# Weight blocks issued at other places of the SyncE queue, and other widths of the column chunks

## The chip, the cores and the metric

The kernel runs on one NeuronCore of one Trainium2 chip. The metric is the device time of one execution in microseconds (us), the median of three runs. A core has TensorE (matrix products), VectorE, ScalarE and GpSimd (elementwise work), and SyncE, which in this kernel only issues transfers. The page of the profile calls them PE (PEld: its weight loads), DVE, ACT, POOL and SP.

## The reference

Chunk-wise attention over 64-token blocks, then an MLP with the SoLU activation and layer norm, then an MLP with PReLU. The change lies in the last part. Cut to it:

```python
# attention and the first MLP give x: 4608 tokens x 512
def _moe2_ref(x, w_in, w_out, alpha):          # d_model 512, d_ff 2048
    h = x @ w_in
    g = np.maximum(h, 0.0) + alpha * np.minimum(h, 0.0)
    return (g @ w_out).astype(np.float32)
```

Everything is float32, and the result has shape 4608 x 512.

## The kernel before, in words

**Phase 1** (`phase1`) computes attention and the first MLP, leaves its result `y` transposed in DRAM (tiles `yd`), and writes the two weights of the second MLP to DRAM in a prepared form (`wid` for `w_in`, `wod` for `w_out`). **Phase 2** (`phase2`) is the second MLP and what the change touches.

Phase 2 forms each matrix product by Strassen's scheme in Winograd's form: both matrices are cut into 2 x 2 quadrants, and seven products of sums of quadrants (`p1` to `p7`) take the place of eight. Each operand is split in a high and a low part, and a product is high*high + high*low + low*high. So each block of a weight holds high and low parts of seven operands: 14336 bytes a partition, 1792 KB a block. Each weight has eight such blocks (`NB2`), tiles `w20` to `w27`. Blocks 0 and 1 lie at the left of the on-chip memory, where room is free early (`NL = 2`), blocks 2 to 7 at the right, in memory that phase 1 holds to its end.

**First product, x @ w_in, with PReLU.** The tokens come as pairs (`PAIRS` = 2304 columns, half of the tokens each side), in six stripes of 384 columns (`SG`, loop `s`). For each stripe the four quadrants of `y` are loaded (`load_y`, four transfers of 384 KB, SyncE queue), and for each of the eight blocks of the weight there is one *unit* (`unit`, loop `b`), 48 in all. A unit runs 7 products of 6 matmuls of 384 columns, in the order p1, p6, p5, p7, p2, p3, p4, in four PSUM banks hx, hy, hz, hv, which alternate between two sets from unit to unit; p2, p3 and p4 accumulate onto hx, hz and hv of the same unit after these have been read. Four results come out, called 22, 11, 12 and 21 in the order in which they are made. Each gets a tile `g` out of a pool of seven (line 787), is passed through PReLU (ScalarE's `ng` and `g`, VectorE's L802) and is stored to DRAM tiles `gd` by SyncE (192 KB each, `store`, L807). The stores of 22 and 11 stand at the end of a unit, those of 12 and 21 in the next unit, behind its second product (`late`). A tile `g` can be written again when its store has landed.

**Second product, g @ w_out.** The 2304 columns are cut in chunks (`CHUNKS`, line 38). A chunk has two groups of products (p1, p5, p6, p7 and then p2, p3, p4), and each group four *pieces* j, two blocks of the weight each. `load_g` loads the quadrants a, b, c, d of a piece (only c and d in the second group); `prepare` forms the sums and splits on ScalarE and VectorE; `multiply` runs one *step*: 12 matmuls of the chunk's width, for one product of one piece. 5 chunks x 28 steps are 140 steps. The first piece (0, 0, 0) is loaded and prepared during the last stripe (tiles `fa` to `fd`, `fhi`, `flo`); the others use pools that reuse the memory of the first product (tiles `ra` to `rd`, `rhi`, `rlo`, `rt`; two buffers each of a to d).

**What sets the order.** All transfers of phase 2 are issued by SyncE, in program order, and go through one hardware queue; ScalarE has another queue for phase 1's stores of `y`. SyncE is in order: a transfer that waits (for its data, for its buffer, or for the transfer eight places back on SyncE's and ScalarE's queues, which shares its semaphore) holds all behind it. In the kernel before, blocks 2 to 7 of the first weight are issued together at the end of phase 1 (line 877), ahead of the y loads of the second stripe and of all stores. In the last stripe, the block of the second weight that takes the place of block b is issued at the end of unit b (line 1027).

Of the kernel before, what the change touches and what calls it, by code (L numbers as in the profile page):

```python
# [34 lines left out]
NS = NT // (2 * SG)  # L35
PAIRS = NT // 2
NB2 = KF2 // 2
CHUNKS = [(0, 256)] + [(p, 512) for p in range(256, PAIRS, 512)]

# [48 lines left out]
def tile_chunk_attention_solu_prelu(  # L90
# [29 lines left out]
    wi_dram = dram.tile([128, NB2, 2, 7, 2, 128], F32, name="wid")  # L120
    wo_dram = dram.tile([128, NB2, 2, 7, 256], F32, name="wod")
# [551 lines left out]
    def add(out, a, b):  # L673
        nc.vector.tensor_tensor(out=out, in0=a, in1=b, op=ALU.add)  # L674
# [7 lines left out]
    def phase2():  # L682
        with ExitStack() as c2:
            def P(name, bufs, side="left", stack=c2, **k):
                return stack.enter_context(tc.tile_pool(name=name, bufs=bufs, side=side, reuse_waits="tile", **k))

            NL = 2
# [9 lines left out]
            def load_w(b, src):  # L697
                W[b] = (wl if b < NL else wr).tile([128, 2, 7, 256], F32R, name=f"w2{b}", tag=f"w{b}")
                if src is wi_dram:
                    nc.sync.dma_start(  # L700
                        out=W[b].bitcast(F32).rearrange("p t i c -> p (t i c)"),
                        in_=src[:, b].rearrange("p t i k c -> p (t i k c)"),
                    )
                else:
                    nc.sync.dma_start(out=W[b].bitcast(F32), in_=src[:, b])
# [15 lines left out]
            def load_y(s):  # L721
                for t in ("11", "12", "22", "21"):
                    r, c = int(t[0]) - 1, int(t[1]) - 1
                    raw[t] = slot(F32 if t == "12" else F32R, f"y{t}")
                    nc.sync.dma_start(
                        out=raw[t].bitcast(F32), in_=y_dram[s][:, 2 * r:2 * r + 2, SG * c:SG * c + SG]
                    )
# [21 lines left out]
            class Unit:  # L749
# [34 lines left out]
                    add(self.v, self.ps["z"], self.u)  # L784

                def f(self, t):
                    self.g[t] = self.tile("g", gp, 7)
                    if t != "11":
                        x, o = {"22": ("v", self.v), "12": ("z", self.u), "21": ("v", self.u)}[t]
                        add(self.g[t], self.ps[x], o)  # L790
# [83 lines left out]
            wr = P("w2r", 1, side="right")  # L874
            ps2.append(P("ps_2r", 1, side="right", space=PSUM))
            gp = P("g2", 1, side="right", stack=ca)
            for b in range(NL, NB2):
                load_w(b, wi_dram)


# [1 line left out]
            GROUPS = (("p1", "p5", "p6", "p7"), ("p2", "p3", "p4"))  # L882
            steps = [(c, g, j, p) for c in range(len(CHUNKS)) for g in range(2) for j in range(4) for p in GROUPS[g]]
            pieces = [(c, g, j) for c in range(len(CHUNKS)) for g in range(2) for j in range(4)]
            start = {x: next(t for t, y in enumerate(steps) if y[:3] == x) for x in pieces}
            src, t4s, ops = {}, {}, {}

            def new(x, tag, dtype=F32R):
                n = CHUNKS[x[0]][1]
                if x == (0, 0, 0):  # L890
                    if tag == "t4":
                        return kp.tile([128, 2, n], dtype, name="t4", tag="t4")
                    return slot(dtype, f"f{tag}")[:, :, :n]
                bufs = dict(t3=1, t2=1, t4=4, hi=4, lo=3).get(tag, 2)
                return rp.tile([128, 2, 512], dtype, name=f"r{tag}", tag=tag, bufs=bufs)[:, :, :n]

            def load_g(x):
                c, g, j = x
                p0, n = CHUNKS[c]
                for tag, t in (("a", "11"), ("b", "12"), ("c", "22"), ("d", "21"))[2 * g:]:  # L900
                    src[x, tag] = new(x, tag, F32 if tag == "b" else F32R)
                    nc.sync.dma_start(
                        out=src[x, tag].bitcast(F32), in_=GD[t][:, 2 * j:2 * j + 2, p0:p0 + n]
                    )
# [13 lines left out]
            def prepare(x, p):  # L918
                a, b, c, d = (src.get((x, t)) for t in "abcd")
                k = x[0], x[2]  # L920
                if p == "p1":
                    low_ = split(x, p, a, a)
                    t3 = src[x, "t3"] = new(x, "t3", F32)
                    dsub(t3, c, b)
                    dsub(b, b, a)
                    low_()
                elif p == "p5":
                    low_ = split(x, p, b, None)
                    t2 = src[x, "t2"] = new(x, "t2", F32)
                    dsub(t2, c, b)  # L930
                    t4 = t4s[k] = new(x, "t4", F32)
                    dsub(t4, d, t2)
                    low_()
                else:
                    f = dict(p6=src.get((x, "t2")), p7=src.get((x, "t3")), p2=d, p3=c, p4=t4s.get(k))[p]
                    split(x, p, f, f if p in ("p2", "p3") else None)()
# [3 lines left out]
            def multiply(t):  # L940
                c, g, j, p = steps[t]
                n = CHUNKS[c][1]
                i, _, key = PRODUCTS[p]
# [12 lines left out]
            def evacuate(t):  # L956
                c, g, j, p = steps[t]
                p0, n = CHUNKS[c]
                while out_:
# [41 lines left out]
            for s in range(NS):  # L1001
                for b in range(NB2):
                    def extra(k):
                        if s + 1 == NS:
                            x = (0, 0, 0)
                            if (b, k) == (0, 3):
                                load_g(x)
                            if k == 2 and 4 <= b:
                                prepare(x, GROUPS[0][b - 4])
                        else:  # L1010
                            if (b, k) == (0, 3):
                                load_y(s + 1)
                            if (b, k) in sums:
                                sum_y(sums[b, k])
                            if (b, k) in early:
                                high_y(s + 1, early[b, k])
                            if (b, k - 1) in early:
                                low_y(s + 1, early[b, k - 1])
                        if s and b == 0:
                            if (8, k) in early:  # L1020
                                high_y(s, early[8, k])
                            if (8, k - 1) in early:
                                low_y(s, early[8, k - 1])

                    prev = unit(s * NB2 + b, s, b, prev, extra)
                    if s + 1 == NS:
                        load_w(b, wo_dram)
            for k in range(3):
                prev.late(k)
# [5 lines left out]
            op = P("o3", 1)  # L1035
            LEAD = 3
            load_g(pieces[1])
            load_g(pieces[2])
            for t in range(4, 4 + LEAD):
                prepare(steps[t][:3], steps[t][3])  # L1040
            for t in range(4, len(steps)):
# [43 lines left out]
```

## Time and profile before

| | |
|---|---|
| median of three runs | 1351.19 us (1347.74 to 1352.4) |
| profiled execution, its own time | 1350.37 us |
| its span, first to last instruction | 1348.6 us |
| TensorE busy | 1271.1 us (94%), mean granted clock 0.976 |
| VectorE, ScalarE, GpSimd busy | 947.5, 689.6, 328.3 us |
| first product's units | 602.3 to 979.6 us of the span |
| second product's steps | 979.5 to 1344.8 us |

The profiled execution lies 0.8 us below the median. Its own time is 1.8 us more than its span. A busy TensorE is not TensorE at its best: matmuls overlap in the records, so lengths are better read from one start to the next. Idle time counts only where the last chain of work runs through it; in phase 2 that is TensorE nearly everywhere. The granted clock is given as a share of 2.4 GHz: 1.0 is full, 0.5 is 1.2 GHz.

### The profile page before, as it was taken

What the parts mean: (1) busy time and instruction counts of PE and PEld (TensorE: products, weight loads), DVE (VectorE), ACT (ScalarE), POOL (GpSimd) and SP (SyncE); (2) the same over time, 40 slices, a digit from 0 to 9 for tenths busy, and PEclk for the clock granted to TensorE, in tenths of its full rate; (3) what the DMA queues carried; (4) which work ended last, traced back from release to release, by engine and by line L of the source; (5) the groups of instructions that cost most, each with busy time, mean ns of one, the idle gap of its engine ahead of it and who ended that gap; (6) DMA issues with size and microseconds to landing.
All of it is one profiled execution on the core that took longest, in us unless ns stands there. A gap on an engine that the chain in (4) does not pass through costs nothing. (4 is left out here: it accounts for less than half of the span.)

```text
span 1348.6 us, 21430 instructions
## 1 busy us (share of the span) xinstructions
PE 1271.1 (94%) x7968; PEld 1157.4 (86%) x7968; DVE 947.5 (70%) x1425; ACT 689.6 (51%) x1140; POOL 328.3 (24%) x309
## 2 busy tenths in 40 slices
PE   4999989999999999994999999999968999999998
PEld 3778779999898889994999999999968888888887
DVE  6986576677777676422777777777756859596783
ACT  5675345555555554332666666666534443444442
POOL 4664254354555643401120202100000000000000
PEclk9799999999999999997999999999978999999999
DMA  9864267576756652539242433436975547483743
GB/s 237 174 158 116 73 165 172 149 172 179 212 165 202 193 170 94 198 113 380 106 159 106 158 124 135 147 112 244 328 247 195 188 151 255 134 274 108 265 134 116
DMA packets 214792, 236.30 MB, mean 175 GB/s; under 512 B 89248, under 2 KB 167072, under 8 KB 212640
## 3 DMA queue, kind: packets, MB, share of 16 engines
q1 hardware_dynamic: 204896, 225.49, 53.5%
q10 hardware_dynamic: 9792, 9.44, 2.1%
q8 instruction: 63, 1.03, 0.3%
q14 instruction: 41, 0.34, 0.1%
HBM read 148.90 MB, written 85.98 MB: 174 GB/s over the span
## 5 line engine op out<-in xcount | busy, mean ns | idle before, releaser
L802 DVE SCALAR_TENSOR_TENSOR g<-ng,nal,g 128x384 f32<-128x384 f32 x192 | 123.6, 644 | 62.2 <-ACT g L680 62.2
L160 PE MATMUL yps<-zh,wo_h 128*128 128x256 f32 x576 | 167.3, 290 | 0.0
L162 PE MATMUL yps<-zh,wo_l 128*128 128x256 f32 x576 | 163.0, 283 | 0.0
L161 PE MATMUL yps<-zl,wo_h 128*128 128x256 f32 x576 | 162.9, 283 | 0.0
L680 ACT ACTIVATE ng<-g 128x384 f32<-128x384 f32 x144 | 75.8, 526 | 150.3 <-DVE g L674 150.3
L763 PE MATMUL hx<-th,w 128*128 128x384 f32 x384 | 113.8, 337 | 16.8 <-ACT s L680 16.8
L763 PE MATMUL hz<-th,w 128*128 128x384 f32 x384 | 114.1, 337 | 2.9 <-DVE wv L674 2.9
L763 PE MATMUL hv<-th,w 128*128 128x384 f32 x384 | 113.7, 336 | 2.6 <-DVE g L674 2.3
L161 PEld LDWEIGHTS yps<-zl,wo_h 128*128 128x128 f32 x576 | 110.5, 192 | 0.1
L160 PEld LDWEIGHTS yps<-zh,wo_h 128*128 128x128 f32 x576 | 110.4, 192 | 0.1
L162 PEld LDWEIGHTS yps<-zh,wo_l 128*128 128x128 f32 x576 | 110.3, 191 | 0.0
L950 PE MATMUL ox<-rhi,w 128*128 128x512 f32 (+1 forms) x312 | 98.1, 379 | 8.3 <-ACT rhi L680 8.3
L950 PE MATMUL oz<-rhi,w 128*128 128x512 f32 (+1 forms) x312 | 96.5, 374 | 0.0
L950 PE MATMUL ov<-rhi,w 128*128 128x512 f32 (+1 forms) x312 | 95.2, 370 | 0.0
L677 POOL TENSOR_TENSOR yt<-y,y 128x384 f32<-128x384 f32 x24 | 28.5, 1208 | 257.7 <-DMA y<-yd 257.7
L680 ACT ACTIVATE rhi<-rt 128x1024 fp32r<-128x1024 f32 (+1 forms) x57 | 56.2, 993 | 65.1 <-DVE rt L677 18.4
L763 PEld LDWEIGHTS hx<-th,w 128*128 128x128 f32 x384 | 71.3, 189 | 17.2 <-ACT s L680 17.2
L481 PE MATMUL h<-wi_h,xh 128*128 128x512 f32 x256 | 72.0, 404 | 8.0 <-ACT xh L467 5.2
L677 DVE TENSOR_TENSOR rlo<-rt,rhi 128x1024 fp32r<-128x1024 f32 (+1 forms) x57 | 64.2, 1137 | 18.1 <-ACT rhi L680 17.9
L680 ACT ACTIVATE g<-g 128x384 f32<-128x384 f32 x144 | 75.2, 522 | 3.1
L950 PEld LDWEIGHTS ox<-rhi,w 128*128 128x128 f32 x312 | 59.3, 195 | 18.7 <-ACT rhi L680 8.5
L763 PEld LDWEIGHTS hz<-th,w 128*128 128x128 f32 x384 | 71.3, 189 | 4.6 <-ACT th L680 4.3
(188 smaller groups left out, 3334.7 us busy)
## 6 DMA issues: line engine op xcount, KB each, us to landing
gd<-g SPq DMA_DIRECT2D x192, 192.0 KB, 1.9
rc<-gd SPq DMA_DIRECT2D x32, 512.0 KB, 4.0
rd<-gd SPq DMA_DIRECT2D x32, 512.0 KB, 5.0
w<-wid SPq DMA_DIRECT2D x8, 1792.0 KB, 14.7
w<-wod SPq DMA_DIRECT2D x8, 1792.0 KB, 9.5
raw<-in_moe_w_out SPq DMA_DIRECT2D x24, 511.8 KB, 3.9
qt<-in_q SPq DMA_DIRECT2D x36, 256.0 KB, 5.2
kbd<-in_k SPq DMA_DIRECT2D x72, 128.0 KB, 5.0
```

What stands on the lines that cost most here:

```text
L160: nc.tensor.matmul(o, lh, rh, start=first, stop=False)
L161: nc.tensor.matmul(o, lh, rl, start=False, stop=False)
L162: nc.tensor.matmul(o, ll, rh, start=False, stop=last)
L481: nc.tensor.matmul(ps[:, n], xh[:, kk], w[:, kk, 512 * n:512 * n + 512], start=(kk == 0 and w is wi_h), stop=False,)
L677: eng.tensor_tensor(out=out, in0=a, in1=b, op=ALU.subtract)
L680: nc.scalar.activation(out=out, in_=in_, func=func, **k)
L763: nc.tensor.matmul(self.ps[x], w[:, a, i, k], d[:, k], start=(p not in CHAINED and k + j == 0), stop=(k == 1 and j == 2), skip_group_check ...
L802: nc.vector.scalar_tensor_tensor(out=self.g[t], in0=self.n[t], scalar=nal_sb[:, f:f + 1], in1=self.g[t], op0=ALU.mult, op1=ALU.add)
L950: nc.tensor.matmul(bank[key, m][:, :n], W[2 * j + k][:, a, i, 128 * m:128 * m + 128], d[:, k], start=(p not in CHAINED and j + k + q == 0) ...
```

## The change

Four edits, all in phase 2:

1. **First weight.** At the end of phase 1 only blocks 2 and 3 are issued. Blocks 4, 5, 6, 7 are issued in units 0, 1, 2, 3 of the first stripe, behind the second product of the unit.
2. **Second weight.** Blocks 0 to 5 stay where they were. Block 6 is issued behind the loads of piece 1, block 7 behind those of piece 2.
3. **Chunks.** The widths 256, 512, 512, 512, 512 become 384, 512, 512, 512, 384.
4. **Pool of results.** `g` has six buffers in place of seven; the first piece, now 384 columns wide, takes more room.

```diff
-CHUNKS = [(0, 256)] + [(p, 512) for p in range(256, PAIRS, 512)]
+CHUNKS = [(0, 384), (384, 512), (896, 512), (1408, 512), (1920, 384)]
...
                 def f(self, t):
-                    self.g[t] = self.tile("g", gp, 7)
+                    self.g[t] = self.tile("g", gp, 6)
...
-            for b in range(NL, NB2):
+            for b in range(NL, NL + 2):
                 load_w(b, wi_dram)
...
                     def extra(k):
+                        if s == 0 and k == 1 and NL + 2 + b < NB2:
+                            load_w(NL + 2 + b, wi_dram)
                         if s + 1 == NS:
...
-                    if s + 1 == NS:
+                    if s + 1 == NS and b < 6:
                         load_w(b, wo_dram)
...
             load_g(pieces[1])
+            load_w(6, wo_dram)
             load_g(pieces[2])
+            load_w(7, wo_dram)
```

What SyncE issues where the first stripe begins, in the kernel before: behind blocks 2 and 3 come blocks 4 to 7 (`w`), the next stripe's `y` and then the stores of unit 0 (`gd`).

```order
L700 DMA w_6748<-wid 128x3584
L700 DMA w_6750<-wid 128x3584
L700 DMA w_6752<-wid 128x3584
L700 DMA w_6754<-wid 128x3584
L725 DMA y_6795<-yd_66 128x2x384
L725 DMA y_6797<-yd_66 128x2x384
L725 DMA y_6799<-yd_66 128x2x384
L725 DMA y_6801<-yd_66 128x2x384
L807 DMA gd_76<-g 128x384
L807 DMA gd_73<-g 128x384
```

The same place in the changed kernel, from block 2 on:

```order
L700 DMA w_6744<-wid 128x3584
L700 DMA w_6746<-wid 128x3584
L700 DMA w_6768<-wid 128x3584
L725 DMA y_6789<-yd_66 128x2x384
L725 DMA y_6791<-yd_66 128x2x384
L725 DMA y_6793<-yd_66 128x2x384
L725 DMA y_6795<-yd_66 128x2x384
L807 DMA gd_76<-g 128x384
L807 DMA gd_73<-g 128x384
L807 DMA gd_74<-g 128x384
L807 DMA gd_75<-g 128x384
L700 DMA w_6860<-wid 128x3584
```

Three blocks in place of six now stand ahead of the first store, and block 5 stands behind the four stores of unit 0.

What SyncE issues where the second product begins, in the kernel before, from the block 6 of the second weight on (`ra` to `rd` are the loads of pieces 1 and 2):

```order
L705 DMA w_10720<-wod 128x3584
L807 DMA gd_74<-g 128x384
L807 DMA gd_75<-g 128x384
L807 DMA gd_76<-g 128x384
L807 DMA gd_73<-g 128x384
L705 DMA w_10805<-wod 128x3584
L807 DMA gd_74<-g 128x384
L807 DMA gd_75<-g 128x384
L902 DMA ra<-gd_73 128x2x256
L902 DMA rb<-gd_74 128x2x256
L902 DMA rc<-gd_76 128x2x256
L902 DMA rd<-gd_75 128x2x256
```

The same place in the changed kernel, from the last two stores on:

```order
L807 DMA gd_74<-g 128x384
L807 DMA gd_75<-g 128x384
L902 DMA ra<-gd_73 128x2x384
L902 DMA rb<-gd_74 128x2x384
L902 DMA rc<-gd_76 128x2x384
L902 DMA rd<-gd_75 128x2x384
L705 DMA w_10883<-wod 128x3584
L902 DMA ra<-gd_73 128x2x384
L902 DMA rb<-gd_74 128x2x384
L902 DMA rc<-gd_76 128x2x384
L902 DMA rd<-gd_75 128x2x384
L705 DMA w_10893<-wod 128x3584
```

No block stands ahead of piece 1 any more, block 6 stands ahead of piece 2 and block 7 ahead of piece 3; the pieces of this chunk are half as wide again.

## Rows read from the trace of the kernel before

**Rows 1.** TensorE in order of time, 594 to 650: start us, us, instruction, [idle before].

```profile
622.35 0.34 PE L763 MATMUL hv<-th,w 128*128 128x384 f32 x1
639.53 0.69 PE L763 MATMUL hx<-th,w 128*128 128x384 f32 x1 [16.84 <-ACT s L680]
```

**Rows 2.** VectorE in order of time, 590 to 640.

```profile
616.58 0.56 DVE L674 TENSOR_TENSOR g<-hv,wv 128x384 f32<-128x384 f32 x1 [3.14 <-DMA yd<-ysb]
637.99 0.56 DVE L674 TENSOR_TENSOR g<-hv,u 128x384 f32<-128x384 f32 x1 [18.09 <-DMA gd<-g]
```

**Rows 3.** SyncE's issues in order of time, three narrow stretches between 603 and 629.

```profile
603.34 0.38 SPq L700 DMA_DIRECT2D w<-wid  x1
...
604.87 0.43 SPq L700 DMA_DIRECT2D w<-wid  x1
...
619.98 8.26 SPq L807 DMA_DIRECT2D gd<-g  x1
```

**Rows 4.** Transfers issued in those stretches: count, KB each, us from issue to landing.

```profile
w<-wid SPq DMA_DIRECT2D x1, 1792.0 KB, 15.2
yd<-ysb ACTq DMA_DIRECT2D x1, 256.0 KB, 13.3
...
w<-wid SPq DMA_DIRECT2D x1, 1792.0 KB, 27.6
...
gd<-g SPq DMA_DIRECT2D x1, 192.0 KB, 17.9
```

**Rows 5.** The page's costliest groups, ScalarE: total us, mean ns, idle before.

```profile
L680 ACT ACTIVATE ng<-g 128x384 f32<-128x384 f32 x144 | 75.8, 526 | 150.3 <-DVE g L674 150.3
```

**Rows 6.** Stretches: length, busy us (x instructions) by engine, clock, DMA share, GB/s.

```profile
625.00:630.00 5.00, 0.00 (x0) 0.00 (x0) 0.00 (x0) 0.00 (x0) 0.00 (x0) 0.64 1.03 442
...
640.00:645.00 5.00, 5.00 (x20) 4.71 (x20) 3.76 (x7) 2.02 (x5) 5.00 (x5) 0.65 0.21 80
...
800.00:900.00 100.00, 98.75 (x566) 97.59 (x565) 76.45 (x135) 64.02 (x134) 18.86 (x16) 1.00 0.39 141
```

**Rows 7.** TensorE in order of time where the second product begins.

```profile
985.10 0.28 PE L950 MATMUL ov<-fhi,w 128*128 128x256 f32 x1
...
993.71 0.58 PE L950 MATMUL ox<-rhi,w 128*128 128x256 f32 x1 [8.34 <-ACT rhi L680]
996.76 0.58 PE L950 MATMUL ox<-ra,w 128*128 128x256 f32 x1 [2.47 <-DVE ra L677]
```

**Rows 8.** The chain that ended last, in order of time: start us, us, what.

```profile
985.88 8.53 DMA rc<-gd
994.50 0.70 DVE rt L677
...
996.76 2.71 PE ox L950 x11
...
1002.03 1.44 PE oy L950 x12
...
1027.86 5.85 DMA rc<-gd
...
1037.67 5.06 PE ox L950 x11
...
1045.61 2.72 PE oy L950 x12
```

**Rows 9.** SyncE's issues, 980 to 985: the last two stores of the first product.

```profile
981.35 1.69 SPq L807 DMA_DIRECT2D gd<-g  x2
```

**Rows 10.** Transfers issued at 1000.2 and at 1033.8.

```profile
rc<-gd SPq DMA_DIRECT2D x1, 256.0 KB, 4.1
...
rc<-gd SPq DMA_DIRECT2D x1, 512.0 KB, 6.5
```

**Rows 11.** VectorE in the third stripe, 740 to 760.

```profile
746.13 0.95 DVE L677 TENSOR_TENSOR tl<-yt,th 128x768 fp32r<-128x768 f32 x1
...
756.03 0.55 DVE L674 TENSOR_TENSOR g<-hz,u 128x384 f32<-128x384 f32 x1
```

**Rows 12.** SyncE's issue at 749.35, and how long that transfer took to land.

```profile
749.35 0.33 SPq L807 DMA_DIRECT2D gd<-g  x1
...
gd<-g SPq DMA_DIRECT2D x1, 192.0 KB, 4.3
```

## The prediction

> **What bounds the kernel now.** I read the page first for the state of TensorE: it is busy for 94% of the span, so only its gaps and the stretches at half clock can be won or lost. The page's forty slices show three places in phase 2 where it is not full; I took TensorE in order of time around each, then the engine that each gap names, back to the transfer behind it.
>
> *Place A, the first stripe.* TensorE ends a product at 622.69 and goes on at 639.53, after 16.84 us on ScalarE's copy `s` [rows 1]. ScalarE waits there for VectorE, and VectorE waited 18.09 us for a store of `g`, until 637.99 [rows 2]: it makes result 21 of unit 1, the eighth of the program, which reuses the first of seven buffers. That first store was issued at 619.98 and landed 17.9 us later, at 637.9 [rows 3, 4]. What it waited for stands ahead of it in the queue: the last block, issued at 604.87, landed at 632.5 [rows 3, 4], then four `y` loads. The clock fell to half inside the gap (mean 0.64 from 625 to 630) and was still 0.65 on the mean from 640 to 645 [rows 6].
>
> *Place B, the second product's start.* The prepared piece's products end at 985.38; with one matmul between, TensorE waits 8.34 and 2.47 us for piece 1 [rows 7]. The chain of waits names its `rc`, issued at 985.88 and landed 8.53 us later [rows 8], behind blocks 6 and 7.
>
> *Place C, the border of chunks 0 and 1.* The chain goes over `rc` of the first 512-wide piece: issued at 1027.86, when its buffer came free, landed 5.85 us later, first full product at 1037.67 [rows 8].
>
> **The change part by part.** The matmuls keep their number and order; what moves is on SyncE.
>
> *A.* Now three blocks stand ahead of the first store. The third was issued at 603.34 and landed after 15.2 us, at 618.5 [rows 3, 4]; nothing ahead of it changes, so I take this over. From the last block's landing to the first store's it was 637.9 - 632.5 = 5.4 us, four `y` loads and the store; the same stands behind block 4 now, so the first store lands at 623.9. With six buffers the result that needs it is the seventh, 12 of unit 1, one result earlier. From VectorE's start to TensorE's it was 639.53 - 637.99 = 1.54 us; now ScalarE has `ng` and `g` of that result to do before, 2 x 0.526 = 1.05 us [rows 5]. TensorE goes on at 623.9 + 1.54 + 1.05 = 626.5, after a gap of 3.8 us. Gain 16.84 - 3.8 = 13.0 us. The clock fell some 3.7 us into the old gap (0.64 over five us is 1.4 us at full), and its return cost about 35% of 5 us, 1.8 us [rows 6]; the new gap ends just there, and I leave this cost in. Ends: 10 us gained if store and `y` loads need 3 us more, 15 if the clock stays.
>
> Blocks 5 to 7 now stand in the stream of stores. A block takes (632.5 - 618.5) / 3 = 4.7 us. Four `y` loads and one store, 1.77 MB, take at most 5.4 us, so the four stores of a unit (0.79 MB) some 2.4 us. Together 7.1 us in a unit of 42 x 0.1745 = 7.3 us (98.75 us busy for 566 matmuls [rows 6]). It just fits: 0, at worst 2 us in each of three units. The blocks come in time: block 5, the earliest needed of them, has four units.
>
> One wait at A stays. VectorE waits 3.14 us, until 616.58, for the last store of phase 1's `y`, whose memory the fifth `g` reuses [rows 2]; that store is on ScalarE's queue and took 13.3 us [rows 4]. The Trainium skill (DMA: Bandwidth & Descriptors, Queues, rings and completion order) says that each DMA engine takes turns between the queues that have work, a packet at a time, so such a store needs neither the whole of SyncE's line nor a free machine. The trace agrees: it landed at about 616.4, long before the last block's 632.5. By that rule it keeps its time, since SyncE's line still holds work until 623.9; if it stood in one line with the blocks, it would have landed after them and would now be earlier. Without the rule the sum has the same 0 here: the fifth of the six `g` still lies on this memory, and what is queued up to 616.4 is the same as before.
>
> *B.* The widths first. 12 matmuls take 1.44 us at 256 columns, 2.72 at 512 [rows 8] and 12 x 0.1745 = 2.09 at 384. The prepared piece has four steps, so it ends 4 x 0.65 = 2.6 us later, at 988.0 on the old scale. Ahead of piece 1 in the queue only stores are left. The last stores are issued until 981.35 + 1.69 = 983.04 [rows 9]; `ra`, `rb`, `rc` follow, `rc` some 0.9 us on, at 983.9. An undisturbed `rc` landed after 4.1 us at 256 KB and 6.5 us at 512 KB [rows 10], so 5.3 at 384 KB: 989.2. Then three VectorE operations: 994.50 to 996.76 at 0.70 us each [rows 8], now 0.95 each [rows 11], so 2.26 + 0.75 = 3.0 us. TensorE starts at 992.2, a gap of 4.2 us against 8.34 + 2.47 = 10.8. Gain 6.6 us. The half clock behind the gap I leave as it was: 996.76 to 1002.03 for 23 matmuls of 0.12 us, 2.5 us lost [rows 8]. Blocks 6 and 7 now stand ahead of pieces 2 and 3: each 4.7 us more for a piece that is due 8.4 us (four steps) after the one ahead. Piece 2: queue free of piece 1 at about 989, block and piece (1.6 MB, some 4.8 us) until 998.5, VectorE 3 us more, 1001.5; due 992.2 + 8.4 + 2.5 = 1003.1. Cost 0; the ends are a loss of all 6.6, and a gain of 9 with no half clock.
>
> *C.* From the freeing of `rc`'s buffer to the full product it took 1037.67 - 1027.86 = 9.8 us, and four short steps covered 4 x 1.44 = 5.8 of it. Four steps of 2.09 cover 8.4. The gap goes from 4.0 to 1.4 us, and I take the clock to hold over it: 11 matmuls took 5.06 us in place of 11 x 0.227 = 2.5 [rows 8]. Gain 2.6 + 2.6 = 5.2 us. Ends: 1 and 6.6.
>
> *Costs.* Widths: per step of all chunks 2 x 2.094 + 3 x 2.72 against 1.44 + 4 x 2.72, 0.03 us, times 28: 0.8 us. The first piece's preparation stands in units 4 to 7 of the last stripe; in two of them three VectorE operations lie between `wv` and result 22, for which TensorE waits, each 0.25 us longer: 1.5 us. Six buffers in the last stripe, where stores land behind blocks: I take 0.7 us, ends 0 and 4. The last chunk's shorter tail is a few tenths, left out.
>
> Sum: -13.0 - 6.6 - 5.2 + 0.8 + 1.5 + 0.7 = -21.8 us, against the profiled execution's 1350.4 us: 1328.6 us. That execution is 0.8 us under the median of the runs, which I don't add; I say 1329.
>
> **The rivals.**
>
> 1. *The blocks between the stores hold them up.* The 7.1 us of transfers per 7.3 us unit speak for it; stores that land 2 us too late in each of three units, with the clock down once more (1.8 us), leave 13.0 - 6 - 1.8 = 5 us of A's gain, and the time is 1337.
> 2. *Blocks 6 and 7 only move the wait from piece 1 to pieces 2 and 3.* For it: the queue was full at B before. Against it: 1.6 us of slack by the sum above. B's 6.6 us are lost and up to 4 more: 1335 to 1340.
> 3. *Six buffers bind every unit; slower.* The third result of a unit needs the first store of the unit before. In the tightest steady place, behind `y` loads, that store was issued at 749.35 and landed at 753.65 [rows 12], and the result is made at 756.03 [rows 11]: 2.4 us to spare. It decides from a landing of 6.7 us. If each of 47 units lost 0.6 us, 28 us would go and the time is 1357. The measured 4.3 us speaks against it outside the stretches with blocks.
> 4. *Nothing changes.* The first store waits as long as before, because what holds it is something other than the blocks. Against it: the landings at A follow each other in the order of issue. Time: 1350.
>
> **How the numbers follow.** The forecast has 0.72, with a range of its own from 1322 to 1335; rival 1 has 0.08, rival 2 0.10, rival 3 0.05, rival 4 0.05. Below the forecast lies the case that the clock falls nowhere, 1.8 + 2.5 us less and a gap shorter: 1322. The range 1320 to 1341 holds the forecast and both rivals that only take part of the gain, and leaves out rivals 3 and 4. No change means within 0.3%, about 4 us, which is what a measurement here can tell. The forecast and rivals 1 and 2 are faster (0.90), rival 4 is the same (0.05), rival 3 is slower (0.05).
>
> **What would show it.** A: VectorE's wait for a store of `g` sits at the seventh result and ends near 624; TensorE's gap is about 4 us; no wait for a block at units 4 to 7. B: `rc` of piece 1 lands some 5 us after its issue; the gap before the ra matmul is near 4 us, and none stands before pieces 2 and 3. C: the gap at the first 512-wide piece is 1 to 2 us at full clock. The forecast is wrong if units in the middle stripes are longer than 7.3 us (rival 3), if TensorE waits in units 2 to 5 of the first stripe (rival 1) or at the steps of pieces 2 and 3 (rival 2).

## The result, and the profile after

The changed kernel takes 1326.72 us (median of 4 runs, 1325.93 to 1328.86) against 1351.10 us before (4 runs beside it, 1347.74 to 1352.40). The ratio is 0.9826, 95% interval 0.9804 to 0.9847: 20.7 to 26.5 us less. The forecast was 1329 us. The profiled execution has a span of 1324.1 us, before 1348.6 us.

**Lining the two traces up.** VectorE's first addition `u` of each unit is a good mark, since there are 48 of them. The difference in its start between the two traces (after less before) goes like this:

| mark | before | after | difference |
|---|---|---|---|
| unit 0 | 604.61 | 601.77 | -2.84 |
| unit 1 | 611.88 | 609.04 | -2.84 |
| unit 2 | 639.72 | 624.88 | -14.84 |
| unit 3 | 647.01 | 632.99 | -14.02 |
| unit 44 | 951.40 | 937.39 | -14.01 |
| unit 45 | 959.74 | 946.53 | -13.21 |
| unit 46 | 967.88 | 955.47 | -12.41 |
| unit 47 | 974.70 | 962.56 | -12.14 |
| last addition `u` of the kernel | 1344.85 | 1320.70 | -24.15 |

So 2.84 us are there before the second phase begins, units 0 to 3 give 11.18, forty-one units in the middle give and take nothing (0.01), the preparation of the wider first piece costs 1.87, and the second product gives 12.01. From the first mark to the last it is 740.24 us before and 718.93 us after. I call this the second phase's time; it is 21.31 us less. It leaves the first phase out, whose length differs from run to run. It has a spread of its own, which stands below the table of the experiments.

*Place A.* TensorE in order of time (start us, us, instruction, idle before):

```profile
614.40 0.44 PE L763 MATMUL hv<-th,w 128*128 128x384 f32 x1 [1.29 <-DVE g L674]
...
624.89 0.69 PE L763 MATMUL hx<-th,w 128*128 128x384 f32 x1 [5.02 <-ACT s L680]
```

VectorE there:

```profile
613.79 0.56 DVE L674 TENSOR_TENSOR g<-hv,wv 128x384 f32<-128x384 f32 x1 [3.20 <-DMA yd<-ysb]
...
621.91 0.56 DVE L674 TENSOR_TENSOR g<-hz,u 128x384 f32<-128x384 f32 x1 [5.80 <-DMA gd<-g]
622.39 1.05 DVE L802 SCALAR_TENSOR_TENSOR g<-ng,nal,g 128x384 f32<-128x384 f32 x1
```

SyncE's issues in that stretch:

```profile
599.61 1.27 SPq L700 DMA_DIRECT2D w<-wid  x3
600.93 3.74 SPq L725 DMA_DIRECT2D y<-yd  x4
606.46 9.72 SPq L807 DMA_DIRECT2D gd<-g  x4
616.88 0.32 SPq L700 DMA_DIRECT2D w<-wid  x1
```

How long the first store and the block at 616.88 took to land (count, KB, us):

```profile
gd<-g SPq DMA_DIRECT2D x1, 192.0 KB, 15.4
...
w<-wid SPq DMA_DIRECT2D x1, 1792.0 KB, 10.6
```

Stretches of five us, the columns as in [rows 6]:

```profile
620.00:625.00 5.00, 0.10 (x1) 0.11 (x1) 2.93 (x5) 2.10 (x5) 5.00 (x6) 0.86 1.08 444
625.00:630.00 5.00, 5.00 (x16) 5.00 (x17) 3.49 (x7) 2.33 (x6) 2.83 (x3) 0.50 1.01 349
630.00:635.00 5.00, 5.00 (x30) 5.00 (x29) 2.86 (x6) 2.13 (x5) 0.00 (x0) 0.96 0.91 323
...
1035.00:1040.00 5.00, 3.75 (x17) 3.05 (x17) 4.97 (x8) 1.44 (x2) 0.00 (x0) 1.00 0.67 244
```

The 16.84 us of [rows 1] are 5.02 now. The result that waits is the seventh, 12 of unit 1 (`g` from `hz` and `u`), where before it was the eighth, from `hv` and `u` [rows 2]. The first store was issued at 606.46 and landed at 621.9. The clock still falls once: 0.86 on the mean from 620 to 625, 0.50 from 625 to 630, 0.96 from 630 to 635.

*Places B and C and the last stripe.* TensorE again:

```profile
942.38 0.44 PE L763 MATMUL hv<-th,w 128*128 128x384 f32 x1 [1.28 <-DVE g L674]
951.33 0.45 PE L763 MATMUL hv<-th,w 128*128 128x384 f32 x1 [1.37 <-DVE g L674]
...
979.74 0.69 PE L950 MATMUL ox<-ra,w 128*128 128x384 f32 x1 [3.85 <-DVE ra L677]
...
1036.38 0.47 PE L950 MATMUL oz<-rhi,w 128*128 128x512 f32 x1 [1.25 <-DVE osb L674]
```

The chain that ended last, at B and at C (start us, us, what):

```profile
971.92 4.63 DMA rc<-gd
...
1023.89 4.44 DMA rc<-gd
```

VectorE in unit 44, and at the border of chunks 0 and 1:

```profile
938.39 0.55 DVE L674 TENSOR_TENSOR wv<-hz,u 128x384 f32<-128x384 f32 x1
938.85 0.95 DVE L677 TENSOR_TENSOR ft<-fc,fb 128x768 f32<-128x768 f32 x1
939.84 0.96 DVE L677 TENSOR_TENSOR fb<-fb,fa 128x768 f32<-128x768 f32 x1
940.90 0.96 DVE L677 TENSOR_TENSOR fa<-fa,fhi 128x768 fp32r<-128x768 f32 x1
941.78 0.55 DVE L674 TENSOR_TENSOR g<-hv,wv 128x384 f32<-128x384 f32 x1
...
1028.42 1.23 DVE L677 TENSOR_TENSOR rt<-rc,rb 128x1024 f32<-128x1024 f32 x1 [2.51 <-DMA rc<-gd]
...
1035.69 1.01 DVE L674 TENSOR_TENSOR osb<-oz,u 128x384 f32<-128x384 f32 x2
```

At B one gap of 3.85 us stands where [rows 7] had 8.34 and 2.47, and none at pieces 2 and 3. At C the first product of the 512-wide piece (`ox`) no longer waits. The 1.25 us stand one product later, at `oz`: VectorE has six operations of the piece's preparation (1028.42 to 1035.7) ahead of `osb`, the addition that frees the bank for `oz`. The first of the six waited 2.51 us for the piece's `rc`, so the chain that ended last still goes over that load, which was issued at 1023.89 and landed 4.44 us later. The clock is 1.00 from 1035 to 1040.

### The profile page after: what moved, and what is told of

The parts are those of the page before. It is cut to its first block, busy times and chain, and to the rows that moved or that the text cites. A ratio compares the mean times of both kernels' runs of the same rounds, so it can differ in the third digit from the quotient of the medians.

```text
span 1324.1 us, 21433 instructions
## 1 busy us (share of the span) xinstructions
PE 1266.7 (96%) x7968; PEld 1167.5 (88%) x7968; DVE 946.5 (71%) x1425; ACT 689.6 (52%) x1140; POOL 328.9 (25%) x309
## 5 line engine op out<-in xcount | busy, mean ns | idle before, releaser
L763 PEld LDWEIGHTS hv<-th,w 128*128 128x128 f32 x384 | 71.3, 189 | 6.6 <-DVE g L674 4.9
L561 DVE TENSOR_TENSOR zl<-zt,zh 128x1024 fp32r<-128x1024 f32 x36 | 44.0, 1222 | 44.0 <-ACT zh L556 44.0
## 6 DMA issues: line engine op xcount, KB each, us to landing
w<-wid SPq DMA_DIRECT2D x8, 1792.0 KB, 10.6
```

Source lines behind the costliest of these rows:

```text
L561: nc.vector.tensor_tensor(out=zl, in0=ps, in1=zh.bitcast(F32), op=ALU.subtract)
L763: nc.tensor.matmul(self.ps[x], w[:, a, i, k], d[:, k], start=(p not in CHAINED and k + j == 0), stop=(k == 1 and j == 2), skip_group_check ...
```

## The experiments

All kernels with their medians, the ratio to runs of the kernel before beside them, the first mark and the second phase's time:

| kernel | median us | ratio, 95% | unit 0 at | second phase |
|---|---|---|---|---|
| before | 1351.10 | | 604.61 | 740.24 |
| changed | 1326.72 | 0.9804 to 0.9847 | 601.77 | 718.93 |
| e1 first weight only | 1336.33 | 0.9874 to 0.9910 | 605.96 | 724.59 |
| e2 second weight only | 1344.77 | 0.9940 to 0.9974 | 604.93 | 736.72 |
| e3 widths, six buffers | 1347.72 | 0.9972 to 0.9999 | 601.59 | 738.86 |
| e4 six buffers only | 1353.34 | 1.0007 to 1.0036 | 605.61 | 741.93 |
| e5 GpSimd prepares | 1326.19 | 0.9802 to 0.9849 | 604.50 | 716.18 |
| e6 one block ahead | 1322.70 | 0.9772 to 0.9809 | 604.74 | 712.36 |
| e7 e5 and e6 | 1321.95 | 0.9760 to 0.9801 | 605.48 | 711.46 |
| e8 no block ahead | 1320.14 | 0.9752 to 0.9793 | 606.00 | 711.27 |
| e9 last stores elsewhere | 1327.77 | 0.9805 to 0.9851 | 610.44 | 714.61 |
| e10 e8 and e9 | 1318.06 | 0.9733 to 0.9782 | 606.11 | 707.74 |
| e11 e10 and e5 | 1316.49 | 0.9719 to 0.9766 | 607.27 | 706.97 |
| e12 e1 and e2 | 1331.07 | 0.9838 to 0.9884 | 604.69 | 723.07 |

How far a time repeats where the code is the same, by the marks of these traces: the changed kernel, e5 and e9 have the same code up to the last stripe, and from unit 1 to unit 3 they need 11.18, 12.50 and 12.43 us less than before. From unit 47 to the end e1 and e4 have the code of before, and need 2.37 and 1.42 us less than it. From unit 4 to unit 39, before, the changed kernel, e1 to e5, e9 and e12 lie within 0.5 us of each other. So a difference of 1 us in units 1 to 3, or of 2 us behind unit 47, shows nothing by itself.

### e1: the first weight's order alone

```diff
 (before)
-            for b in range(NL, NB2):
+            for b in range(NL, NL + 2):
...
+                        if s == 0 and k == 1 and NL + 2 + b < NB2:
+                            load_w(NL + 2 + b, wi_dram)
```

> Only the first edit: two blocks of the first weight ahead, one per unit between the stores; old widths, seven buffers, old order of the second weight. Theory (the gain in unit 1 stands by itself): TensorE's wait in unit 1 is about 5.0 us (16.8 before), from unit 3 to unit 47 the units follow each other as before, the waits at the start of the second product are unchanged (10.8 us and 3.6 us), time 11 below before: 1340. Rival (the 2.8 us by which the second phase began earlier in the trace of the changed kernel also belong to this edit, since four blocks fewer are issued at the end of the first phase): the first addition of the second phase at about 601.8 here and at about 604.6 in the kernels that lack the edit, time 14 below before: 1337. Rival (blocks between stores hold them up): further waits in units 2 to 5, 1345 or more.

TensorE, and VectorE's wait behind it:

```profile
627.69 0.44 PE L763 MATMUL hx<-th,w 128*128 128x384 f32 x1 [3.60 <-ACT s L680]
```

```profile
626.14 0.56 DVE L674 TENSOR_TENSOR g<-hv,u 128x384 f32<-128x384 f32 x1 [4.85 <-DMA gd<-g]
```

The mark moves by 13.36 us against before from unit 1 to unit 3, and stays (by 0.08) to unit 47: blocks between stores hold nothing up. The first addition is at 605.96, so the earlier start in the changed kernel's trace is not this edit's. The wait is 3.60 and not the 5.0 expected, and the result that waits is the eighth, as it was before. The changed kernel gains 11.18 us there with six buffers, e5 and e9 gain 12.50 and 12.43: the seventh buffer is worth 0.9 to 2.2 us. The second phase is 15.65 us shorter than before, but 2.37 of these lie behind unit 47, where nothing was edited.

### e2: the second weight's order alone

```diff
 (before)
-                    if s + 1 == NS:
+                    if s + 1 == NS and b < 6:
...
             load_g(pieces[1])
+            load_w(6, wo_dram)
             load_g(pieces[2])
+            load_w(7, wo_dram)
```

> Only the second edit: the last two blocks of the second weight behind the loads of pieces 1 and 2; widths, buffers and the first weight's order as before. Theory: piece 0 is still 256 wide, so TensorE's wait for piece 1 falls from 10.8 us to about 6.4 us (3.85 us in the changed kernel, where piece 0 covers 2.6 us more), pieces 2 and 3 do not wait, time 4 to 5 below before: 1346.5. Rival (the two blocks only move the wait to pieces 2 and 3): waits of 4 us or more there, time 1350 to 1352.

TensorE from piece 1 on; the rows at 999.54 and 1006.87 are pieces 2 and 3:

```profile
987.01 0.38 PE L950 MATMUL ox<-rhi,w 128*128 128x256 f32 x1 [1.01 <-ACT rhi L680]
991.29 0.58 PE L950 MATMUL ox<-ra,w 128*128 128x256 f32 x1 [3.90 <-DVE ra L677]
999.54 0.39 PE L950 MATMUL ox<-ra,w 128*128 128x256 f32 x1 [0.36 <-DVE ra L677]
...
1006.87 0.39 PE L950 MATMUL ox<-ra,w 128*128 128x256 f32 x1 [0.83 <-DVE ra L677]
```

The wait for piece 1 is 4.9 us in place of 10.8 in the trace of before, and 0.36 and 0.83 us come up at pieces 2 and 3: the rival's wait is there, but small. The second phase is 3.5 us shorter, the median ratio says 3.5 to 8. Behind unit 47 the trace needs 3.8 us less than before, but only 1.5 and 2.4 less than e1 and e4, so the size of this gain is known only to some 2 us.

### e3: the widths and the six buffers

```diff
 (before)
-CHUNKS = [(0, 256)] + [(p, 512) for p in range(256, PAIRS, 512)]
+CHUNKS = [(0, 384), (384, 512), (896, 512), (1408, 512), (1920, 384)]
...
-                    self.g[t] = self.tile("g", gp, 7)
+                    self.g[t] = self.tile("g", gp, 6)
```

> Only the third and fourth edits: the widths 384, 512, 512, 512, 384 and six buffers; both weights' orders as before. Theory: TensorE's wait at the end of the first chunk falls from 3.6 us to about 1.3 us with the clock granted in full (5 us gained with the half clock that goes), the first piece covers 2.6 us more of the wait for piece 1 (about 8.2 us left of 10.8), the preparation of the wider piece costs 1.9 us in units 4 to 7 of the last stripe, the two chunks of 384 cost 1.4 us; in sum 4 to 5 below before: 1346.5. Rival (six buffers bind): units of more than 7.28 us in every stripe, 1351 or more. Rival (the widths pay only together with the new order of the second weight): the wait for piece 1 stays near 10.8 us, 1350.

TensorE in unit 1 and at piece 1:

```profile
638.29 0.69 PE L763 MATMUL hx<-th,w 128*128 128x384 f32 x1 [18.62 <-ACT s L680]
...
995.81 0.69 PE L950 MATMUL ox<-rhi,w 128*128 128x384 f32 x1 [6.71 <-ACT rhi L680]
1000.08 0.69 PE L950 MATMUL ox<-ra,w 128*128 128x384 f32 x1 [3.58 <-DVE ra L677]
```

Only 1.4 us of the 4 to 5 came (second phase; the ratio says 0.1 to 3.8). The wait for piece 1 is 10.3 us, not 8.2: its loads stand behind blocks 6 and 7, and here the second rival held. And the wait in unit 1 is 18.62 us where before has 16.84. At C 0.66 us are left, at `oz` as in the changed kernel. The middle units keep their time (0.08 us from unit 4 to unit 39), so six buffers do not bind every unit.

### e4: six buffers alone

```diff
 (before)
-                    self.g[t] = self.tile("g", gp, 7)
+                    self.g[t] = self.tile("g", gp, 6)
```

> Only the fourth edit: six buffers for the results instead of seven. Theory: no change, 1351; the units of all stripes are spaced as before and the two small waits in the last stripe (0.48 and 0.59 us) stay. Prediction's own term: 0.7 us in the last stripe, 1351.8. Rival (six buffers bind every unit): 7 us or more, 1357.

TensorE, and VectorE's wait behind the first of the rows:

```profile
642.77 0.69 PE L763 MATMUL hx<-th,w 128*128 128x384 f32 x1 [19.09 <-ACT s L680]
...
959.70 0.44 PE L763 MATMUL hv<-th,w 128*128 128x384 f32 x1 [0.75 <-DVE g L674]
```

```profile
639.52 0.56 DVE L674 TENSOR_TENSOR g<-hz,u 128x384 f32<-128x384 f32 x1 [19.61 <-DMA gd<-g]
```

The mark loses 2.85 us against before from unit 1 to unit 3, nothing more to unit 43, and 0.30 us in unit 44. So neither 0 nor 0.7 in the last stripe: the price is in unit 1. TensorE stops at the same point as before (642.77 - 19.09 is 622.7 on the clock of before, as there), but from VectorE's start on the waiting result to TensorE's it is now 3.25 us (639.52 to 642.77) in place of 1.54, since the seventh result waits and not the eighth.

### e5: GpSimd prepares the first piece

```diff
 (changed kernel, in prepare)
+                eng = nc.gpsimd if x == (0, 0, 0) else nc.vector
...
-                    dsub(t3, c, b)
+                    dsub(t3, c, b, eng)
```

The same for the subtractions into `b`, `t2` and `t4`.

> The changed kernel, but the four subtractions of piece 0's preparation in the last stripe that need no split value (two of three in unit 4, two of three in unit 5) are done by GpSimd, which is idle there, instead of VectorE. Theory (the preparation of the wider piece holds the results of units 4 and 5 up on VectorE, 1.28 and 1.37 us of TensorE's time): both waits gone, units 44 to 47 spaced as all others, 1.9 below the changed kernel: 1324.8, or 1.1 per 1000 more off before. Rival (GpSimd's subtractions are so slow, some 1.8 us each by its 1.2 us for 128x512, that the last step of each preparation holds VectorE in order as much as now): no change, 1326.7.

VectorE while GpSimd works, and GpSimd:

```profile
917.79 1.46 DVE L802 SCALAR_TENSOR_TENSOR g<-ng,nal,g 128x384 f32<-128x384 f32 x1
...
921.52 1.78 DVE L802 SCALAR_TENSOR_TENSOR g<-ng,nal,g 128x384 f32<-128x384 f32 x1 [1.15 <-ACT g L680]
923.23 0.55 DVE L674 TENSOR_TENSOR g<-hz,u 128x384 f32<-128x384 f32 x1
923.70 1.73 DVE L802 SCALAR_TENSOR_TENSOR g<-ng,nal,g 128x384 f32<-128x384 f32 x1
```

```profile
916.79 2.05 POOL L677 TENSOR_TENSOR ft<-fc,fb 128x768 f32<-128x768 f32 x1 [48.77 <-PE hy L763]
...
921.04 1.85 POOL L677 TENSOR_TENSOR ft<-fc,fb 128x768 f32<-128x768 f32 x1
922.97 2.04 POOL L677 TENSOR_TENSOR t<-fd,ft 128x768 f32<-128x768 f32 x1
```

TensorE in unit 1, where this kernel and the changed kernel are the same:

```profile
627.45 0.69 PE L763 MATMUL hx<-th,w 128*128 128x384 f32 x1 [4.91 <-ACT s L680]
```

The waits of 1.28 and 1.37 us are gone, two of 0.58 and 0.27 us come up in unit 40, four units earlier, where GpSimd now works, and from unit 39 to unit 47 the mark gains 1.85 us on the changed kernel, as expected. The wait for piece 1 grows from 3.85 to 4.73 us (0.22 and 4.51), which is half of the gain; by the marks 0.31 us are lost behind unit 47. The second phase is 2.75 us shorter than the changed kernel's, but 1.32 of these lie in units 1 to 3, ahead of the edit. The medians cannot tell this from no change.

### e6: one block ahead in place of two

```diff
 (changed kernel)
-            for b in range(NL, NL + 2):
+            for b in range(NL, NL + 1):
...
-                        if s == 0 and k == 1 and NL + 2 + b < NB2:
-                            load_w(NL + 2 + b, wi_dram)
+                        if s == 0 and k == 1 and NL + 1 + b < NB2:
+                            load_w(NL + 1 + b, wi_dram)
```

> The changed kernel with one block of the first weight issued ahead of the units instead of two, the others again one per unit, so one unit later each. Theory (the first store of a result lands late because three blocks and four loads of 7 MB in all are queued ahead of it): one block of 1.8 MB fewer is 4.2 us at the 427 GB/s of that stretch; TensorE's wait of 5.0 us in unit 1 falls to about 0.8 us, the wait for the store of ysb (1.3 us) goes with it, the clock stays full, no block is late: 6 us below the changed kernel, 1320.5. Rival (the stores wait on SyncE for the y loads, not for the blocks): the wait stays at 4 us or more, 1326. Rival (a block comes late): a wait at the start of unit 3, 4 or 5.

TensorE in unit 2, and the stretch around it:

```profile
622.65 0.45 PE L763 MATMUL hx<-th,w 128*128 128x384 f32 x1 [1.38 <-ACT s L680]
624.28 0.44 PE L763 MATMUL hz<-th,w 128*128 128x384 f32 x1 [0.29 <-DVE wv L674]
```

```profile
620.00:625.00 5.00, 3.33 (x18) 2.68 (x17) 4.62 (x8) 2.45 (x6) 5.00 (x5) 1.00 0.99 411
```

1.67 us of waits are left of 6.31 (1.29 and 5.02), the clock is 1.00 from 620 to 625, and no block is late. The second phase is 6.57 us shorter than the changed kernel's, the median 4.0 us. In units 1 to 3 the mark gains 6.0 us on the changed kernel, 4.7 on e5 and e9. What holds the first store back is the blocks ahead of it, not the `y` loads.

### e7: both

The edits of e5 and e6 together.

> The changed kernel with both: one block ahead, and the four subtractions on GpSimd. Theory (both waits are independent): the sum of the two, 8 us below the changed kernel, 1318.5. Rival: only one of them counts, 1320.5 to 1325.

Second phase 711.46 us, 7.47 less than the changed kernel's and 0.90 less than e6's. Up to unit 47 the mark is 1.89 us ahead of e6, the preparation's full share; 0.99 of it is lost again behind. So about half of the preparation's gain is kept, and the medians of e6 and e7 cannot be told apart.

### e8: no block ahead

```diff
 (changed kernel)
-            for b in range(NL, NL + 2):
-                load_w(b, wi_dram)
...
-                        if s == 0 and k == 1 and NL + 2 + b < NB2:
-                            load_w(NL + 2 + b, wi_dram)
+                        if s == 0 and k == 1 and NL + b < NB2:
+                            load_w(NL + b, wi_dram)
```

> The changed kernel with no block of the first weight ahead of the units: block b is issued in unit b - 2. Theory: only one block is ahead of the first store; the waits of unit 1 are gone as with one block ahead (the first store has 4 us more than it needs), and block 3, issued behind the first stores at about 616, lands at about 626 and is needed at 623 by unit 3: a wait of 2 to 4 us there with some half clock; 1322 to 1325. Rival (blocks land fast enough since little is queued): as with one block ahead, 1320.5.

TensorE's only wait in the first stripe's units, and two of VectorE's:

```profile
654.99 0.44 PE L763 MATMUL hx<-th,w 128*128 128x384 f32 x1 [0.17 <-DMA w<-wid]
```

```profile
647.82 0.56 DVE L674 TENSOR_TENSOR g<-hz,u 128x384 f32<-128x384 f32 x1 [0.77 <-DMA gd<-g]
...
655.54 0.56 DVE L674 TENSOR_TENSOR g<-hz,u 128x384 f32<-128x384 f32 x1 [0.54 <-DMA gd<-g]
```

The rival held: unit 1 has no wait at all, unit 3 none, and a block is late by 0.17 us once. The mark loses 1.1 us from unit 5 to unit 7, more than this row. The mark is VectorE's, and VectorE waits there 0.77 and 0.54 us for stores of `g`; TensorE itself, from the first `hy` of unit 5 (641.10) to that of unit 7 (656.15), needs only 0.5 us more than two units of 7.28. The second phase is 7.66 us shorter than the changed kernel's, 1.09 shorter than e6's.

### e9: the last two stores on ScalarE's queue

```diff
 (changed kernel, in late, k == 2)
-                        self.store("12")
-                        self.store("21")
+                        last = nc.scalar if self.s + 1 == NS and self.b + 1 == NB2 else None
+                        self.store("12", last)
+                        self.store("21", last)
```

`store` issues on the engine that it is given, else on SyncE.

> The changed kernel, but the last two stores of the last unit are issued from ScalarE's queue, so that the loads of piece 1 on SyncE's queue no longer stand behind them. Theory (the wait of 3.85 us for piece 1 is the loads' late issue: the third is issued at 971.9, behind a store whose result is ready at 970.4, though its buffer is free when the last unit's products end at 967): the loads go out some 4 us earlier, TensorE's wait is under 1 us, the half clock behind it goes: 6 us below the changed kernel, 1320.5. Rival (the loads are bound by what the DMA engines still have to move, blocks of the second weight and stores): the wait stays at 3 us or more, 1326.

TensorE at piece 1:

```profile
985.71 0.44 PE L951 MATMUL ox<-ra,w 128*128 128x384 f32 x1 [2.55 <-DVE ra L677]
988.50 0.45 PE L951 MATMUL oz<-rlo,w 128*128 128x384 f32 x1 [0.41 <-DVE rlo L677]
```

and in unit 1, where this kernel too is the same as the changed kernel:

```profile
633.53 0.69 PE L763 MATMUL hx<-th,w 128*128 128x384 f32 x1 [4.92 <-ACT s L680]
```

A miss by half. Measured from unit 47's mark, `rc` is issued 2.2 us earlier than in the changed kernel (977.12 less 970.01, against 971.92 less 962.56), but it now takes 5.4 us to land in place of 4.6, with the two stores beside it, so the rival, by which the loads are bound by what the DMA engines still have to move, is not excluded. The wait is 2.96 us and the clock no longer falls behind it (1.00 from 980 to 990; the changed kernel has 0.50 from 980 to 985). The second phase is 4.32 us shorter; of these, 1.25 lie in units 0 to 3, ahead of the edit. The median shows no gain. In the profiled execution, the longest of the five, the first phase is 8.7 us longer than in the changed kernel's; how long it was in the other four is not known, so why the median shows no gain stays open.

### e10 and e11: the gains together

e10 has the edits of e8 and e9, e11 those of e5 besides.

> The changed kernel with no block of the first weight ahead of the units (each two units before its use) and the last two stores on ScalarE's queue. Theory: the two gains add: 6 us below the kernel with no block ahead alone (1320.1): 1314. Rival: 1320.

> As the kernel before it, and the four subtractions of piece 0's preparation on GpSimd. Theory: the last stripe's two waits (1.28 and 1.37 us) go, and since the wait for piece 1 is now short, little of it is given back there: 1.5 us further, 1312.5. Rival (piece 0 ends earlier and the wait for piece 1 grows by as much, as it did by 0.9 of 1.9 us before): 1314.

e10 is 3.5 us shorter in the second phase than e8 alone, where 6 were expected; 2.75 of these lie behind unit 47 (the wait for piece 1 is 2.92 us). e11 has 0.77 us more, half of the theory's 1.5. Its 1316.49 us are the best time here, 34 us under before (ratio 0.9719 to 0.9766), 10 under the changed kernel.

### e12: both orders without the widths

The edits of e1 and e2 together, on the kernel before: the changed kernel without its other widths and with seven buffers.

> The first two edits together, without the other widths and with seven buffers. Theory (the edits add up; six buffers cost 2 us in unit 1, since a seventh would let one more result be written before the first store has landed): TensorE's wait in unit 1 is 3.6 us as with the first edit alone, and from the first addition of the second phase to the last of the kernel it takes 721 us (718.9 in the changed kernel, 740.2 before): 1329. Rival (the widths and six buffers bring nothing once both orders are changed): 1326.7 or less.

TensorE in unit 1 and at C:

```profile
626.62 0.69 PE L763 MATMUL hx<-th,w 128*128 128x384 f32 x1 [3.74 <-ACT s L680]
...
1021.27 0.50 PE L950 MATMUL ox<-ra,w 128*128 128x512 f32 x1 [3.90 <-DVE ra L677]
```

The wait in unit 1 came as expected, the time 2 us over. From unit 1 to unit 3 the mark gains 2.16 us on the changed kernel (0.9 on e5 and e9, which have six buffers too), from unit 44 to unit 47 another 1.9 (the narrow preparation), and from unit 47 to the end it loses 7.9 (3.90 us at C, and small waits at pieces 2 and 3). The other widths, with the six buffers that they force, are worth 4.1 us net between these two executions, 4.4 by the medians.

## Why the prediction was right

The forecast of 1329 us is 2.3 us above the median, and its sum of -21.8 us stands against 21.31 us in the second phase. The mechanism held at A and B; that the sum is met to 0.5 us is in part luck, since A came out 1.8 us short and the second product 1.0 us over, and both have a spread of that size between executions of the same code. The rest of the difference in the medians, some 3 us, lies in the first phase, whose length (unit 0 at 601.6 to 610.4 in fourteen executions) goes with no edit: e1, which has the first edit, begins at 605.96, and e3, which lacks it, at 601.59.

| step | forecast | measured |
|---|---|---|
| A, to unit 3, with six buffers | -13.0 | -11.2 (-12.5 in e5, -12.4 in e9; -13.4 with seven, e1) |
| blocks between the stores | 0 | 0.01 (unit 3 to unit 44) |
| preparation and six buffers, last stripe | +1.5 + 0.7 = +2.2 | +1.9 (of it buffers alone 0.3, e4) |
| B, C and widths | -6.6 - 5.2 + 0.8 = -11.0 | -12.0 (-9.6 and -10.6 against e1 and e4, which have the code of before there) |
| sum | -21.8 | -21.3 |

**A, the mis-sized term.** Place and result were right: the seventh result waits, for the first store. The step that came out too good is "TensorE goes on at 623.9 + 1.54 + 1.05 = 626.5, after a gap of 3.8 us. Gain 16.84 - 3.8 = 13.0 us". On the clock of the second trace (2.84 us earlier) the store was forecast for 621.1 and landed at 621.9. From VectorE's start to TensorE's it was 2.98 us and not 2.59, because VectorE's operation of line 802 took 1.05 us while GpSimd was busy for all of 620 to 625. The gap became 5.02 us, and of the 11.8 us gained on it 0.6 went to the half clock behind it. That gives the 1.8 us by which A fell short in this execution. The gap repeats (4.91 us in e5, 4.92 in e9); the half clock does not: from unit 2 to unit 3 the changed kernel needs 8.11 us, e5 and e9 need 6.97 and 6.90. There A fell short by 0.5 and 0.6 us.

**What six buffers cost.** I put 0.7 us into the last stripe for them and 1.05 into A. In the last stripe it is 0.3 us (e4), the rest is in unit 1. From unit 1 to unit 3 the kernels with seven gain 13.36 us (e1) and 13.34 (e12) on before, those with six 11.18 (the changed kernel), 12.50 (e5) and 12.43 (e9). So the price there is 0.9 us in two executions, near the 1.05 of the sum, and 2.2 in one; in the old order of the first weight it is 2.5 (e3) and 2.9 (e4). What repeats, in the new order, is the longer gap: 4.91 to 5.02 us with six, 3.60 and 3.74 with seven. In e1 the store lands at the same time (626.14, on the changed kernel's clock 621.95), and TensorE goes on 1.55 us behind VectorE, as I had it for seven buffers, in place of 2.98. What differs, also between executions of the same code, is the half clock behind the gap: unit 2 to unit 3 takes 8.11, 6.97 and 6.90 us with six, 7.33 and 7.14 with seven.

**The store of ysb.** The prediction left its wait where it was, and the changed kernel has it (1.29 us of TensorE, 13.4 us to land, 13.3 in [rows 4]). But that it keeps its time while SyncE's line holds work does not hold: in e6 it landed after 11.6 us, at 614.8, though the first store of `g` on SyncE's queue landed only at 619.5, and in e8 after 7.7 us, and TensorE's wait was gone in both. The Trainium skill (DMA: Bandwidth & Descriptors, Queues, rings and completion order) has the DMA engines take turns between queues; these runs show that beside a shorter line on the other queue a store of 256 KB still lands sooner.

**Preparation.** Three operations between `wv` and result 22, as the prediction said: 938.85 to 941.7 in unit 44, and TensorE waits 1.28 and 1.37 us; beside the narrower operations of before it waited 0.48 and 0.59. Each of the two units lost 0.8 us where 0.75 were forecast.

**B and C.** `rc` landed 4.63 us after its issue (5.3 forecast), the gap is 3.85 (4.2), pieces 2 and 3 wait for nothing. That needs both edits: blocks moved without the width leave 0.36 and 0.83 us there (e2), the width without the blocks leaves 10.3 us at piece 1 (e3). At C the size (1.25 us at full clock, 1.4 forecast) was right by luck. The forecast had TensorE's wait at the piece's first product, from a load of 5.85 us. The load took 4.44 us, and that product did not wait; the 1.25 us stand at the second, behind `osb` on VectorE, whose operations begin when the load has landed. In the other kernels with the new widths this wait is 0.56 to 0.78 us.

**The rivals.** Blocks between stores holding them up: no wait in units 2 to 7. Blocks 6 and 7 moving the wait to pieces 2 and 3: a trace of it in e2, none with the wider piece. Six buffers in every unit: no, units 3 to 44 keep their time. Nothing changes: no.

## What to carry to other kernels

Count what stands ahead of the first small transfer that an engine waits for, not only whether the large ones come in time: with six blocks ahead of the first store TensorE waited 16.84 us, with three 5.02, with two 1.67 (e6), with one not at all (e8), and no block held TensorE up by more than 0.84 us (e11). Before a buffer is given up, look for the place where results outrun their stores, and price it from the landing of the store to the slowest engine's next start, the clock behind it included. Where the time from run to run is dominated by another stage, compare marks inside the trace, and first look how far they repeat where the code is the same: within 0.5 us in the middle units here, but by 1.3 us across a fall of the clock in unit 1 and by 2.4 us in the second product, while the intervals of the medians are 3.6 to 6.6 us wide.

## What the runs showed of the hardware

VectorE's operation with both tiles in SBUF (line 802, 0.62 us) took 1.46 to 1.78 us while GpSimd ran subtractions of 1.85 to 2.05 us, and the additions that read a bank of PSUM kept their 0.55 us (e5, rows at 921.52 and 923.23). The Trainium skill (GPSIMD Engine Reference, Specifications) says that GpSimd's way into SBUF is shared with VectorE, and that instructions of VectorE with two SBUF inputs contend; the rows agree, and the price here is 0.8 to 1.2 us for each. Each of the three ended 0.41 or 0.42 us after the subtraction beside which it began (919.25 after 918.84, 923.30 after 922.89, 925.43 after 925.01), so on these rows it finishes only when that subtraction has ended.

A gap's length alone did not say whether the granted clock falls. Behind 5.02 us it was 0.50 in the next stretch, that is 1.2 GHz (625 to 630 in the changed kernel). Gaps of 1.38 us (e6), 2.55 us (e9) and 2.92 us (e10) left it at 1.00, while one of 2.58 us (e11) was followed by 0.70 from 975 to 980, and one of 2.45 us (e4, place C) by 0.66 from 1040 to 1045.
